# Depthwise-separable 1x1 layer on one core: the second weight load moves to ScalarE's queue, and the fourth weight piece is evicted by two engines

## The chip, the cores and the metric

The kernel runs on one core of one Trainium2 chip. The metric is device time in microseconds (us). Before the change three runs took 573.55, 574.01 and 574.22 us; their median is 574.01 us.

## The reference

x is a 1x384x384x384 image in bf16 (384 channels), dw a depthwise filter with a 1x1 window, pw a 384x384 matrix. With a window of one, the reference is

```python
out = x * dw[0, 0][None, None, None, :]       # one factor per channel
return jnp.einsum('bhwc,cd->bhwd', out, pw)
```

So the kernel computes x · (diag(dw) · pw), with x taken as 147,456 rows of 384 channels. The factor of each channel can be put into the weights once, ahead of the rows.

## The kernel before

**The rows.** The 147,456 rows are cut into 288 supertiles of 512 rows. Chunks of 1 to 10 supertiles are loaded by SyncE's queue (`load_x`, L121; the DMA is issued at L133) into three buffers X. The first chunks hold one supertile each (384 KB), so that the first can start early. VectorE transposes each supertile into T (L364 for the first half of the very first one, in three steps; L366 for all others). TensorE multiplies T by the weights w_r into a PSUM tile of four banks (`supertile`, L212; the matmul is at L222, 48 of them for a supertile). ScalarE evicts the PSUM tile into O (L426), and SyncE's queue stores O (L173). Two T tiles and two PSUM tiles, PS[0] and PS[1], alternate.

**The weights.** Before the first supertile the weights have to be built. w_r holds diag(dw) · pw with its rows in the order that the transposes give. dw (768 bytes) is loaded by ScalarE's queue (L178), and pw by SyncE's queue in two transfers: rows 0 to 127 (L179, 96 KB, semaphore s_pw) and rows 128 to 383 (L180, 192 KB, s_pw2). The first x chunk follows behind them on the same queue (L181, issued at L133). TensorE runs matmuls on constants while it waits (`idle_work`, L239), spreads dw over the partitions with three matmuls (L252), and VectorE copies the result (L394) and multiplies a selection matrix by it (L397), once for each k, which counts up s_sw.

Then TensorE makes the weights in six pieces i = 0 to 5, with k = i // 2 the 128 rows of pw and r = i % 2 (the loop at L263 to L280; the matmul is at L272). A piece is one pair of matmuls, v = 0 and 1, each into a PSUM bank of its own, and counts up s_w. The two pieces of k = 2 run their pair twice (`times`, L262). The pieces 0, 1, 4 and 5 lie in PS[1], the pieces 2 and 3 in PS[0] (`w_ps`, L206). Before k = 0 TensorE waits for s_pw, before k = 1 for s_pw2 (L265), and before each piece of k = 2 for the eviction of the piece that lies in the same banks (L269).

**The evictions of the weights.** `w_out` (L379) copies a piece of 128x768 from PSUM into w_r at L382: VectorE takes piece 1, ScalarE the pieces 0, 2, 3, 4 and 5, as `w_eng` (L175) says. s_wr[0] counts VectorE's, s_wr[1] ScalarE's.

**What the first supertile waits for.** It writes PS[0], where the pieces 2 and 3 have been. `w_first` (L204) makes TensorE wait for pieces 0 to 3 before step (0, 0), for piece 4 before step (4, 0) and for piece 5 before step (4, 1). Step (0, 0) also waits for the first transpose of L364, and that for the first x chunk.

**Order on the engines.** On ScalarE: the load of dw, the activation table and two tiny copies (L338), the evictions of the weights, then one eviction (L426) for each supertile. On VectorE: L387, L394, L397, the eviction of piece 1, then the transposes. GpSimd waits for all of w_r (`w_all`), then copies parts of it (L330) for the last supertile alone.

Of the kernel before, what the change touches and what calls it, by code (L numbers as in the profile page):

```python
# [26 lines left out]
def kernel(  # L27
# [12 lines left out]
    nc = tc.nc  # L40
    P = nc.NUM_PARTITIONS
    B, H, W, C = x.shape
# [31 lines left out]
    pw_n = raw[:, 0 : 3 * D].rearrange("p (k d) -> p k d", d=D)  # L74
# [4 lines left out]
    w_r = consts.tile([P, NB, 2, D], BF16, name="w_r")  # L79
# [25 lines left out]
    s_pw2 = nc.alloc_semaphore("s_pw2")  # L105
# [5 lines left out]
    s_wr = [nc.alloc_semaphore(f"s_wr{e}") for e in range(2)]  # L111

    with tc.tile_critical(sync_engine=mybir.EngineType.Pool, no_gpsimd_drain=True) as section:
# [7 lines left out]
        def load_x(t, eng=nc.sync):  # L121
            g, i, off, first, L = chunks[t]
            dst, sem, _ = x_of(t)
            rows = xf[512 * first : 512 * (first + L), :]
            if first + 3 < NS:
                src = rows.rearrange("(p s) c -> p (s c)", p=P)
                dst = dst.rearrange("p s c -> p (s c)")
                if i == 0 and g >= NR:
                    je = g_end[g - NR]
                    eng.wait_ge(s_t[je % 2][1], je // 2 + 1)  # L130
            else:
                src = rows.rearrange("(a k q) c -> q a k c", k=4, q=4)
            eng.dma_start(dst, src).then_inc(sem, 16)  # L133
# [38 lines left out]
            eng = nc.scalar if first + 1 == NS and k == 2 else nc.sync  # L172
            eng.dma_start(dst, src).then_inc(s_o[g % NR], 16)  # L173

        w_eng = [1, 0, 1, 1, 1, 1]  # L175
        w_all = [(s_wr[e], w_eng.count(e)) for e in range(2)]

        nc.scalar.dma_start(dw_row[:], dw.rearrange("a e c -> a (e c)")).then_inc(s_dw, 16)  # L178
        nc.sync.dma_start(pw_n[:, 0], pw[0:P, :]).then_inc(s_pw, 16)  # L179
        nc.sync.dma_start(pw_n[:, 1:3], pw[P:C, :].rearrange("(k p) d -> p k d", p=P)).then_inc(s_pw2, 16)  # L180
        load_x(0)  # L181

        todo = []
# [15 lines left out]

        w_done = [(s_wr[e], w_eng[: i + 1].count(e)) for i, e in enumerate(w_eng)]

        w_first = {(0, 0): [(0, 1), (1, 3)], (4, 0): [(1, 4)], (4, 1): [(1, 5)]}  # L204

        def w_ps(i):  # L206
            return PS[0 if i in (2, 3) else 1][:, 2 * (i % 2) : 2 * (i % 2) + 2, :D]
# [4 lines left out]
        def supertile(s, rv):  # L212
            for b, par in steps:
                for q in range(4):
                    if q == 0 and par == 0 and b in (0, 3):
                        nc.tensor.wait_ge(s_t[s][b // 3], rv)
                    if q == 0 and s == 0:
                        for e, v in w_first.get((b, par), []):
                            nc.tensor.wait_ge(s_wr[e], v)
                        if par == 0 and b in (1, 2):  # L220
                            nc.tensor.wait_ge(s_tb, b)
                    mm = nc.tensor.matmul(  # L222
                        PS[s][:, q, :D],
                        lhsT=Ts[s][32 * q : 32 * q + 32, b, par::2],
                        rhs=w_r[32 * q : 32 * q + 32, b, par, :],
                        start=(b, par) == steps[0],
                        stop=(b, par) == steps[-1],
                        tile_position=(32 * q, 0),
                    )
                    if (b, par) == steps[0] and q == 0:  # L230
                        mm._wait_ge(s_a[s], rv)
                    if (b, par) in ((2, 1), (5, 1)) and q == 3:
                        mm.then_inc(s_pe)
# [29 lines left out]
        for k in range(3):  # L263
            if k == 1:
                nc.tensor.wait_ge(s_pw2, 16)  # L265
            nc.tensor.wait_ge(s_sw, k + 1)
            for r in range(2):
                if k == 2:
                    nc.tensor.wait_ge(*w_done[r])  # L269

                for v in [0, 1] * times.get((k, r), 1):
                    mm = nc.tensor.matmul(  # L272
                        PS[(k + 1) % 2][:, 2 * r + v, :D],
                        lhsT=sel_w[64 * v : 64 * v + 64, k, r, :, :].rearrange("p q w -> p (q w)"),
                        rhs=pw_n[64 * v : 64 * v + 64, k, :],
                        start=True,
                        stop=True,
                        tile_position=(64 * v, 0),
                    )
                mm.then_inc(s_w)  # L280
        with nc.tensor.Fori(0, NS // 2 - 1, 1) as it:
            rv = nc.tensor.to_reg(it + 1)
            for s in range(2):
                supertile(s, rv)
        supertile(0, NS // 2)

        Tk = Ts[1][:].rearrange("p b (i r) -> p (b i) r", r=2)
# [15 lines left out]
        for m in range(4):  # L303
# [14 lines left out]
            out=eye[:],  # L318
            in_=ones[:, 0:P],
# [20 lines left out]
        def transposes(t, j):  # L340
            g, i, off, first, L = chunks[t]
            jj = first + j
            s = jj % 2
            if jj + 1 == NS:
                nc.vector.wait_ge(s_xk, 32)
                Tw = Ts[s][:].bitcast(U32).rearrange("p b (m w) -> p (b m) w", w=32)
                for v in range(2):
                    blocks = slice(12 * v, 12 * v + 12)
                    ins = nc.vector.transpose(out=Tw[:, blocks], in_=Xk[:, blocks].bitcast(U32))  # L349
                    ins._wait_ge(s_pe, 2 * (jj - 2) + v + 1)  # L350
                    ins.then_inc(s_t[s][v])
                return
            X, sem, n = x_of(t)
            Xw = X.bitcast(U32).rearrange("p (k l) c -> p k l c", l=L)
            Tw = Ts[s][:].bitcast(U32).rearrange(
                "p b (k i) -> p b k i" if t < 2 else "p b (i k) -> p b k i", k=4
            )
            for h in range(2):
                if h == 0 and j == 0:
                    nc.vector.wait_ge(sem, n)  # L360
                if h == 0 and jj == 0:
                    for b in range(3):
                        x_b = Xw[:, :, 0, 32 * b : 32 * b + 32]
                        nc.vector.transpose(out=Tw[:, b], in_=x_b).then_inc(s_tb if b else s_t[0][0])  # L364
                    continue
                ins = nc.vector.transpose(  # L366
                    out=Tw[:, 3 * h : 3 * h + 3],
                    in_=Xw[:, :, j, 96 * h : 96 * h + 96].rearrange("p k (b w) -> p b k w", w=32),
                )
                if jj >= 2:  # L370
                    ins._wait_ge(s_pe, 2 * (jj - 2) + h + 1)
                ins.then_inc(s_t[s][h])
# [3 lines left out]

        order = [(t, j) for t in range(NT) for j in range(chunks[t][4])]

        def w_out(i):  # L379
            e, k, r = w_eng[i], i // 2, i % 2  # L380
            out, in_ = w_r[:, 2 * k : 2 * k + 2, r, :], w_ps(i)
            o = nc.vector.tensor_copy(out, in_) if e == 0 else nc.scalar.copy(out, in_)  # L382
            o._wait_ge(s_w, i + 1)
            o.then_inc(s_wr[e])
# [3 lines left out]
            out=sel[:],  # L388
            in_=eye[:].rearrange("p (v w r) -> p r w v", v=2, r=2),
# [6 lines left out]
        for k in range(3):  # L396
            nc.vector.tensor_scalar_mul(  # L397
                sel_w[:, k], sel[:].unsqueeze(2).to_broadcast([P, 2, 4, 32]), dw_f[:, k : k + 1]
            ).then_inc(s_sw)
        for i in range(6):  # L400
            w_out(i)
        transposes(*order[0])
        transposes(*order[1])

        for jj, (t, j) in enumerate(order):
            g, i, off, first, L = chunks[t]
# [32 lines left out]
        for o in sorted(range(NR), key=lambda o: (len(groups) - 1 - o) % NR):  # L439
            n = sum(n_parts[t] for t, c in enumerate(chunks) if c[0] % NR == o)  # L440
# [36 lines left out]
```

## Time and profile before

| what | value |
|---|---|
| runs, median (lowest to highest) | 574.01 us (573.55 to 574.22) |
| the profiled execution's own time | 573.57 us |
| span of its profile, first to last instruction | 571.8 us |
| granted TensorE clock | 1.00 |
| TensorE matmul busy | 566.9 us (99%) |
| VectorE busy | 507.7 us (89%) |
| ScalarE busy | 418.7 us (73%) |
| GpSimd busy | 13.9 us (2%) |
| moved by DMA | 226.88 MB, mean 397 GB/s |

The profile shows one execution. Its times are counted from the first instruction of the span. PE is TensorE's matmul, PEld its weight load, DVE VectorE, ACT ScalarE, POOL GpSimd; SPq and ACTq are the issues of DMAs by SyncE and ScalarE. In a row of the timeline the first number is the start, the second the duration, and behind the operation stands, in brackets, how long the engine sat idle before it and what ended that. Times are in us unless ns is said. A matmul's duration reaches from its start to its modelled end, so that durations of matmuls overlap; the distance between starts tells the pace.

### The profile page before, as it was taken

What the parts mean: (1) busy time and instruction counts of PE and PEld (TensorE: products, weight loads), DVE (VectorE), ACT (ScalarE), POOL (GpSimd) and SP (SyncE); (2) the same over time, 40 slices, a digit from 0 to 9 for tenths busy, and PEclk for the clock granted to TensorE, in tenths of its full rate; (3) what the DMA queues carried; (4) which work ended last, traced back from release to release, by engine and by line L of the source; (5) the groups of instructions that cost most, each with busy time, mean ns of one, the idle gap of its engine ahead of it and who ended that gap; (6) DMA issues with size and microseconds to landing.
All of it is one profiled execution on the core that took longest, in us unless ns stands there. A gap on an engine that the chain in (4) does not pass through costs nothing.

```text
span 571.8 us, 29716 instructions
## 1 busy us (share of the span) xinstructions
PE 566.9 (99%) x13843; PEld 414.2 (72%) x13843; DVE 507.7 (89%) x588; ACT 418.7 (73%) x298; POOL 13.9 (2%) x41
## 2 busy tenths in 40 slices
PE   9999999999999999999999999999999999999997
PEld 5777777777777777777777777777777777777775
DVE  7888989989989989989989889889889889889885
ACT  6777777777777777777777777777777777777775
POOL 2042000000000000000000000000000000000000
PEclk9999999999999999999999999999999999999999
DMA  8999999999999999999999999999999999998677
GB/s 317 441 385 385 428 430 432 437 421 414 427 441 422 427 384 422 403 381 392 433 393 383 414 414 406 412 399 420 420 375 435 386 392 397 416 396 361 283 287 260
DMA packets 28085, 226.88 MB, mean 397 GB/s; under 512 B 1450, under 2 KB 7851, under 8 KB 24107
## 3 DMA queue, kind: packets, MB, share of 16 engines
q1 hardware_dynamic: 27140, 225.91, 97.5%
q10 hardware_dynamic: 934, 0.89, 0.4%
q14 instruction: 10, 0.07, 0.0%
q8 instruction: 1, 0.02, 0.0%
HBM read 113.54 MB, written 113.25 MB: 397 GB/s over the span
## 4 chain that ended last, share of the span: by engine, by line
PE 99%; issue 0%; ACT 0%
PE ps L222 98%; PE ps L272 0%; PE ps L239 0%; PE ps L307 0%; PE ps L295 0%; ACT O L421 0%; PE ps L252 0%
## 5 line engine op out<-in xcount | busy, mean ns | idle before, releaser
L222 PE MATMUL ps<-w_r,T 32*128 32x384 bf16 x13776 | 559.8, 321 | 0.1
L366 DVE STREAM_TRANSPOSE T<-X 128x384 uint32<-128x384 uint32 x571 | 499.8, 877 | 55.0 <-PE ps L222 1.1
L222 PEld LDWEIGHTS ps<-w_r,T 32*128 32x128 bf16 x13776 | 411.4, 93 | 148.6 <-issue 0.6
L426 ACT CAST O<-ps 128x1536 bf16<-128x1536 f32 x286 | 411.7, 1440 | 146.4 <-PE ps L222 146.4
L336 POOL COPY Xk<-Xl 32x256 bf16<-32x256 bf16 x16 | 6.3, 396 | 0.0
L335 POOL COPY Xk<-Xl 32x128 bf16<-32x128 bf16 x16 | 4.6, 290 | 25.6 <-DMA Xl<-in_x_dram 24.7
L382 ACT CAST w_r<-ps 128x768 bf16<-128x768 f32 x5 | 3.6, 818 | 0.8 <-PE ps L272 0.8
L330 POOL COPY raw<-w_r 32x768 bf16<-32x768 bf16 x4 | 3.3, 821 | 6.4 <-ACT w_r L382 6.2
L239 PE MATMUL ps<-const-bfloat16-1.0 32*128 32x384 bf16 x24 | 2.2, 516 | 1.1 <-PEq L461 1.1
L272 PE MATMUL ps<-raw 64*128 64x384 bf16 x16 | 2.8, 498 | 0.1
L272 PEld LDWEIGHTS ps<-raw 64*128 64x128 bf16 x16 | 0.8, 114 | 2.2 <-DMA raw<-in_pw_dram 1.2
L338 ACT ACT_TABLE_LOAD x1 | 1.3, 1283 | 1.5 <-PEq L461 1.5
L417 DVE CAST O<-ps 128x384 bf16<-128x384 f32 x2 | 1.0, 552 | 1.4 <-PE ps L222 1.4
L366 DVE STREAM_TRANSPOSE T<-Xl 128x384 uint32<-128x384 uint32 x2 | 1.8, 876 | 0.2
L239 PEld LDWEIGHTS ps<-const-bfloat16-1.0 32*128 32x128 bf16 x24 | 0.7, 117 | 1.5 <-issue 1.5
L387 DVE TENSOR_REDUCE sel<-eye 128x64 f32<-128x128 bf16 x1 | 0.3, 288 | 1.5 <-POOL eye L317 1.5
L349 DVE STREAM_TRANSPOSE T<-Xk 128x384 uint32<-128x384 uint32 x2 | 1.2, 578 | 0.5 <-PE ps L222 0.4
L421 ACT CAST O<-ps 128x384 bf16<-128x384 f32 x2 | 1.0, 479 | 0.7 <-PE ps L307 0.7
L307 PE MATMUL ps<-raw,T 128*128 128x384 bf16 x8 | 1.5, 327 | 0.0
L382 DVE CAST w_r<-ps 128x768 bf16<-128x768 f32 x1 | 1.0, 958 | 0.5 <-PE ps L272 0.5
L364 DVE STREAM_TRANSPOSE T<-X 128x128 uint32<-128x128 uint32 x3 | 0.7, 283 | 0.6 <-DMA X<-in_x_dram 0.6
L421 DVE CAST O<-ps 128x384 bf16<-128x384 f32 x2 | 1.1, 558 | 0.1
(14 smaller groups left out, 5.4 us busy)
## 6 DMA issues: line engine op xcount, KB each, us to landing
X<-in_x_dram SPq DMA_DIRECT2D x25, 3840.0 KB, 22.2
out_dram<-O SPq DMA_DIRECT2D x25, 3840.0 KB, 28.1
X<-in_x_dram SPq DMA_DIRECT2D x3, 1536.0 KB, 18.8
X<-in_x_dram SPq DMA_DIRECT2D x2, 1920.0 KB, 15.7
out_dram<-O SPq DMA_DIRECT2D x2, 1920.0 KB, 24.4
out_dram<-O SPq DMA_DIRECT2D x2, 1536.0 KB, 13.3
X<-in_x_dram SPq DMA_DIRECT2D x6, 384.0 KB, 5.2
out_dram<-O SPq DMA_DIRECT2D x3, 768.0 KB, 6.1
```

What stands on the lines that cost most here:

```text
L222: mm = nc.tensor.matmul(PS[s][:, q, :D], lhsT=Ts[s][32 * q : 32 * q + 32, b, par::2], rhs=w_r[32 * q : 32 * q + 32, b, par, :], start=(b, ...
L239: nc.tensor.matmul(PS[0][:, 2 * (i % 2) + i // 2, :D], lhsT=ones[32 * i : 32 * i + 32, 0:P], rhs=ones[32 * i : 32 * i + 32, :], start=True ...
L272: mm = nc.tensor.matmul(PS[(k + 1) % 2][:, 2 * r + v, :D], lhsT=sel_w[64 * v : 64 * v + 64, k, r, :, :].rearrange("p q w -> p (q w)"), rhs ...
L307: mm = nc.tensor.matmul(PS[1][:, m, :D], lhsT=Tk[:, P * (m + 2) : P * (m + 3), par], rhs=w_k[:, par, :], start=False, stop=par == 1,)
L330: nc.gpsimd.tensor_copy(w_k[quads[n]], w_r[quads[n], n]).then_inc(s_wk)
L335: nc.gpsimd.tensor_copy(Xk[quads[n], g:8:4, :], x_b).then_inc(s_xk)
L336: nc.gpsimd.tensor_copy(Xk[quads[n], 8 + g : 24 : 4, :], Xl[quads[g], :, 64 * n : 64 * n + 64]).then_inc(s_xk)
L338: nc.scalar.copy(warm[:, s : s + 1], nc.const_aps.tensor(0.0, [P, 1], F32)).then_inc(s_a[s])
L366: ins = nc.vector.transpose(out=Tw[:, 3 * h : 3 * h + 3], in_=Xw[:, :, j, 96 * h : 96 * h + 96].rearrange("p k (b w) -> p b k w", w=32),)
L382: o = nc.vector.tensor_copy(out, in_) if e == 0 else nc.scalar.copy(out, in_)
L421: o = (nc.scalar.copy if n % 2 else nc.vector.tensor_copy)(Ov[:, n, j, :], PS[s][:, n, :D])
L426: a = nc.scalar.copy(Ov[:, :, j, :], PS[s][:, :, :D])
```

## The change

Two things are changed. The second load of pw is issued by ScalarE's queue, behind dw, and no longer by SyncE's between the first load of pw and the first x chunk. And the fourth piece of the weights (i = 3) is evicted in two halves of one PSUM bank each, the first by ScalarE, the second by VectorE; the counts on which TensorE and GpSimd wait are worked out from the new list.

```diff
-        w_eng = [1, 0, 1, 1, 1, 1]
-        w_all = [(s_wr[e], w_eng.count(e)) for e in range(2)]
+        w_units = [(0, 0, 2, 1), (1, 0, 2, 0), (2, 0, 2, 1), (3, 0, 1, 1), (3, 1, 2, 0), (4, 0, 2, 1), (5, 0, 2, 1)]
+
+        def w_after(i):
+            n = [sum(u[3] == e and u[0] <= i for u in w_units) for e in range(2)]
+            return [(s_wr[e], n[e]) for e in range(2)]
+
+        w_all = w_after(5)
 
         nc.scalar.dma_start(dw_row[:], dw.rearrange("a e c -> a (e c)")).then_inc(s_dw, 16)
         nc.sync.dma_start(pw_n[:, 0], pw[0:P, :]).then_inc(s_pw, 16)
-        nc.sync.dma_start(pw_n[:, 1:3], pw[P:C, :].rearrange("(k p) d -> p k d", p=P)).then_inc(s_pw2, 16)
+        nc.scalar.dma_start(pw_n[:, 1:3], pw[P:C, :].rearrange("(k p) d -> p k d", p=P)).then_inc(s_pw2, 16)
         load_x(0)
...
-        w_done = [(s_wr[e], w_eng[: i + 1].count(e)) for i, e in enumerate(w_eng)]
-
-        w_first = {(0, 0): [(0, 1), (1, 3)], (4, 0): [(1, 4)], (4, 1): [(1, 5)]}
+        w_first = {(0, 0): w_after(3), (4, 0): w_after(4)[1:], (4, 1): w_after(5)[1:]}
...
-                        for e, v in w_first.get((b, par), []):
-                            nc.tensor.wait_ge(s_wr[e], v)
+                        for sem, v in w_first.get((b, par), []):
+                            nc.tensor.wait_ge(sem, v)
...
-                    nc.tensor.wait_ge(*w_done[r])
+                    nc.tensor.wait_ge(*w_after(r)[1 - r])
...
-        def w_out(i):
-            e, k, r = w_eng[i], i // 2, i % 2
-            out, in_ = w_r[:, 2 * k : 2 * k + 2, r, :], w_ps(i)
+        def w_out(i, v0, v1, e):
+            k, r = i // 2, i % 2
+            out, in_ = w_r[:, 2 * k + v0 : 2 * k + v1, r, :], w_ps(i)[:, v0:v1]
...
-        for i in range(6):
-            w_out(i)
+        for u in w_units:
+            w_out(*u)
```

A unit is (piece, first bank, last bank + 1, engine), with engine 0 VectorE and 1 ScalarE.

## The prediction, made before the result was known

> **What bounds the kernel now.** I read the page first (its groups), then the chain that ended last, then the timeline of each engine over the first 9 us in narrow windows, then the DMA view in windows. First the page's group of the main matmul and the chain:
>
> ```profile
> span 571.8 us, 29716 instructions
> L222 PE MATMUL ps<-w_r,T 32*128 32x384 bf16 x13776 | 559.8, 321 | 0.1
> ```
>
> ```profile
> 1.12 1.49 PE ps L239 x13
> ...
> 4.86 1.33 PE ps L272 x8
> 6.19 0.07 issue
> 6.26 559.83 PE ps L222 x13776
> ```
>
> The group's last number is TensorE's idle time ahead of these 13,776 matmuls: 0.1 us in all. From 6.26 to 566.09 nothing but TensorE's own pace counts (559.83 / 13,776 is 0.0406 us each, 0.1625 for four). The change touches only what lies ahead of 6.26. So the question is one: when does the first L222 start? Whatever it moves by moves the end by the same.
>
> Who ends last ahead of 6.26? The weights: ACT's and DVE's evictions, the first transpose, and PE's pairs of L272.
>
> ```profile
> 3.91 0.80 ACT L382 CAST w_r<-ps 128x768 bf16<-128x768 f32 x1 [0.80 <-PE ps L272]
> 4.61 0.80 ACT L382 CAST w_r<-ps 128x768 bf16<-128x768 f32 x1
> 5.30 0.82 ACT L382 CAST w_r<-ps 128x768 bf16<-128x768 f32 x1
> ```
>
> ```profile
> 4.23 0.96 DVE L382 CAST w_r<-ps 128x768 bf16<-128x768 f32 x1 [0.48 <-PE ps L272]
> 5.81 0.31 DVE L364 STREAM_TRANSPOSE T<-X 128x128 uint32<-128x128 uint32 x1 [0.62 <-DMA X<-in_x_dram]
> ```
>
> ```profile
> 3.37 0.82 PE L272 MATMUL ps<-raw 64*128 64x384 bf16 x4
> 3.96 0.87 PE L272 MATMUL ps<-raw 64*128 64x384 bf16 x4
> 4.86 0.82 PE L272 MATMUL ps<-raw 64*128 64x384 bf16 x4
> 5.45 0.74 PE L272 MATMUL ps<-raw 64*128 64x384 bf16 x4
> ```
>
> Three things end almost together: piece 3 is in w_r at 5.30 + 0.82 = 6.12, the first transpose is done at 5.81 + 0.31 = 6.12, and PE's last pair is issued at 5.77 (a row below), which at the pairs' distance of 0.32 frees PE at 6.09. The change is aimed at the first two. The third stands 0.17 behind 6.26. That is all that can be won, 0.03% of the time.
>
> **The change, part by part.**
>
> *The halves.* Single-bank evictions stand at the kernel's end:
>
> ```profile
> L421 ACT CAST O<-ps 128x384 bf16<-128x384 f32 x2 | 1.0, 479 | 0.7 <-PE ps L307 0.7
> L421 DVE CAST O<-ps 128x384 bf16<-128x384 f32 x2 | 1.1, 558 | 0.1
> ```
>
> ACT's half would end at 5.30 + 0.48 = 5.78 instead of 6.12. DVE's half starts behind piece 1 (4.23 + 0.96 = 5.19) and takes 0.56, to 5.75; DVE lay idle there (the 0.62 in the row at 5.81), so it costs nothing as long as x is not there before. Alone, this part wins 0.34 for piece 3 and, with the 6.12 of the transpose and the 6.09 of PE beside it, next to nothing for the start. ACT's pieces 4 and 5 come 0.34 earlier; steps (4, 0) and (4, 1) do not wait for them now, as the 0.1 us of idle says. GpSimd's copies (L330) feed only the end of the kernel.
>
> *The queues.* Before, with ACT's first compute instruction:
>
> ```profile
> 0.97 0.39 SPq L179 DMA_DIRECT2D raw<-in_pw_dram  x1
> 1.42 0.41 SPq L180 DMA_DIRECT2D raw<-in_pw_dram  x1
> 1.88 0.46 SPq L133 DMA_DIRECT2D X<-in_x_dram  x1
> ```
>
> ```profile
> 0.97 0.53 ACTq L178 DMA_DIRECT2D dw_row<-in_dw_dram  x1
> 1.54 1.28 ACT L338 ACT_TABLE_LOAD   x1 [1.54 <-PEq L461]
> ```
>
> ```profile
> raw<-in_pw_dram SPq DMA_DIRECT2D x1, 192.0 KB, 2.5
> X<-in_x_dram SPq DMA_DIRECT2D x1, 384.0 KB, 3.9
> ```
>
> Without L180 on SP, the first x chunk is issued at 1.42, 0.46 earlier, and so are the x chunks behind it. On ACT the load of pw comes behind dw at 0.97 + 0.53 = 1.50, 0.08 later than before, and takes 0.41 to 0.53. It pushes the table load and the two small copies by 0.4 to 0.5; ACT was idle for 0.80 ahead of its first eviction at 3.91, so 0.3 is left and nothing is lost. dw itself stays first.
>
> *What the new queue does to the transfer* is the term that decides. Before, pw's 192 KB stood ahead of all x in one queue and landed at 1.42 + 2.5 = 3.92; k = 1 started at 3.96, just as PE came free. Now pw's packets are in ACT's queue and x's are in SP's, ready at the same moment. How the 16 DMA engines share two queues is seen later in this trace, where Xl (ACT's queue, 384 KB) meets a long transfer of SP's. The DMA view of 28 to 31 us, and the wait that it ended:
>
> ```profile
> q1 hardware_dynamic: 40, 1.23, 97.6%
> q10 hardware_dynamic: 42, 0.06, 5.7%
> ```
>
> ```profile
> 24.05 0.42 ACTq L137 DMA_DIRECT2D Xl<-in_x_dram  x1
> ```
>
> ```profile
> 35.87 0.29 POOL L335 COPY Xk<-Xl 32x128 bf16<-32x128 bf16 x1 [24.75 <-DMA Xl<-in_x_dram]
> ```
>
> 40 packets of SP's queue (q1, 30 KB each) against 42 of ACT's (q10, 1.5 KB each): one for one, whatever their size. 384 KB took 11.8 us in that company, against 3.9 for the first x chunk. For pw: 256 rows of 768 bytes (k = 1 and 2 over 128 partitions) are 256 packets, 16 for each engine. An x chunk of one supertile is 128 packets of 3 KB, 8 for each engine. So pw lands when 16 x packets of each engine have gone between, the whole first and second chunk. Their pace, from three DMA windows, 1.8 to 2.5, 2.5 to 3.5 and 4.5 to 7.0 us:
>
> ```profile
> q1 hardware_dynamic: 128, 0.09, 50.2%
> ...
> DMA packets 295, 0.23 MB, mean 233 GB/s; under 512 B 22, under 2 KB 285, under 8 KB 295
> ...
> DMA packets 315, 0.85 MB, mean 339 GB/s; under 512 B 39, under 2 KB 39, under 8 KB 315
> ```
>
> The 128 packets of the first pw load are all begun by 2.5. Of the second window, 285 - 22 = 263 packets are pw's: 16.4 for each engine in 1 us, 0.06 each. Of the third, 315 - 39 = 276 are x's: 17.25 in 2.5 us, 0.145 each. A pair costs 0.145 + 0.06 = 0.205; the low end is 0.175 (the small one half hidden beside the large), the high end 0.22. 16 pairs from 2.5 take 3.3 us (2.8 to 3.5), and the last packets, begun by 3.5, landed at 3.92, so 0.4 more. pw then lands at 6.1 to 6.2 (5.7 to 6.4) instead of 3.92. I take 6.15: 2.2 us later.
>
> *From there.* Call the start of k = 1 T = 6.2. PE has six pairs left (two of k = 1, four of k = 2), none of which waits for an eviction any more, since pieces 0 and 1 are long in w_r. At 0.32 they are through at T + 1.92 = 8.12. ACT: piece 2 starts at T + 0.6 and its half of piece 3 0.7 later, done at T + 1.8. DVE: its half starts when piece 3 is made, T + 0.9, done T + 1.45, the transpose T + 1.75 (x, after 8 pairs, landed at 2.5 + 1.65 + 0.4 = 4.55). So PE's pairs end last, all three within 0.2, and the halves save 0.2 that the unsplit piece 3 would have cost. First L222: 8.1 instead of 6.26, **+1.85**.
>
> *The clock.* The matmuls' pace changes once in the trace, though the granted clock is shown as 1.00 throughout:
>
> ```profile
> 5.45 0.55 PE L272 MATMUL ps<-raw 64*128 64x384 bf16 x2
> ...
> 5.77 0.42 PE L272 MATMUL ps<-raw 64*128 64x384 bf16 x2
> ```
>
> A matmul of 384 columns takes 0.52 up to here, then 0.4, and 0.32 at L222, where pairs' pace has doubled. It happens at about 5.8, 4.7 us after the first matmul at 1.12. The new wait leaves PE idle from 3.37 + 0.82 = 4.19 to 6.2. Nothing in the trace shows a matmul after an idle stretch like that, so two bounds. If the full pace comes at 5.8 all the same, the six pairs go at half the distance, the evictions set the start at about T + 1.65, and 0.25 is won back. If the 4.7 us count anew from T, full pace comes at 10.9, and the L222 from 8.1 to 10.9 run at half pace: 1.4 lost. I take the middle, **+0.5**. [...]
>
> *Sum.* 1.85 + 0.5 = +2.35, from the profiled execution's 573.57 (span 571.8 and 1.77 around it) 575.9. That execution lies 0.44 under the median of 574.01, at the lower end of its runs; on the median the sum is 576.3, which I forecast. Its own range is 575.1 (pw at 5.7, clock as before: +1.35 - 0.25 = +1.1) to 577.5 (+2.1 + 1.4).
>
> **Rivals.**
>
> *A. pw is not held up* (it enters the engines before x does, or the sharing is kinder at the start than at 28 us). Then the change does what it says: x lands at 5.35, DVE's half ends at 5.75, the transpose at 6.06, and PE's 6.09 sets the start: -0.17, 573.85, no slower. It decides up to a delay of 0.3: k = 2 starts at 4.86 for ACT's piece 0 (3.91 + 0.80), and k = 1 could end 0.3 later without being noticed. For it: both loads are issued within 0.1 us. Against it: 16 packets need 1 us even alone, and x's stand ready all that time.
>
> *B. The engines take longer turns than one packet*, so that pw's 16 packets of an engine go through in one turn, behind the first x chunk: 2.5 + 8 x 0.145 + 16 x 0.06 + 0.4 = 5.0, first L222 at 5.05 + 1.92 = 7.0, +0.7, 574.7 (with the clock between 574.5 and 575.3). Against it: the 40 to 42. [...]
>
> *C. x gets a whole chunk's lead.* It is issued 0.08 ahead of pw. If the engines take x's first 8 packets before pw's first, 24 of x's pass before pw lands, not 16: 8 x 0.145 = 1.2 more, +3.5 with the clock's middle and +4.4 with its upper bound, 577.5 to 578.4. Against it: the first x packets stand behind the first pw load until 2.5, so that 0.08 should be lost there.
>
> **How the numbers follow.** The forecast has 0.74, A 0.10, B 0.10, C 0.06. The range for 8 in 10 takes in the forecast's own (575.1 to 577.5) and B: 574.5 to 577.5; A and C stay outside. A measurement of this kernel can tell about 0.2%, 1.15 us, from no change; slower by more means over 575.16. That is nearly all of the forecast, all of C and a little of B: 0.78. Within 0.2%: A, most of B and the edge of the forecast: 0.21. Faster by over 0.2%: no case reaches it, 0.01.
>
> **What the profile after would show.** Right: the weight load ahead of k = 1 waits over 1.5 us for pw's DMA; pw's 192 KB take 4.0 to 5.0 from issue to landing; ACTq's packets stand one for one against SPq's in the first 6 us; the first x chunk lands before pw; the first L222 starts at 7.7 to 8.5; the group of L222 lasts 559.8 or up to 1.4 more. Wrong: k = 1 still starts at about 4.0 (A), or at about 5 (B); or L222 shows idle time of its own, so that something behind the start has changed, which I exclude above.

## The result and the profile after

Six runs of the changed kernel took 575.16 to 577.31 us, median 576.10; six of the kernel before, beside them, 573.55 to 574.22, median 573.86. The ratio is 1.0042 with a 95% interval of 1.0028 to 1.0055: 1.6 to 3.2 us slower. The profiled execution took 575.75, 2.18 more than that of before.

The page's first line and main group, and the chain that ended last:

```profile
span 574.0 us, 29717 instructions
L225 PE MATMUL ps<-w_r,T 32*128 32x384 bf16 x13776 | 560.7, 321 | 0.0
```

```profile
1.53 4.00 DMA raw<-in_pw_dram
5.53 0.05 issue
5.58 2.10 PE ps L275 x12
7.68 560.59 PE ps L225 x13304
```

The main matmul stands at L225 now, that of the weights at L275. The chain, which before began with TensorE's own matmuls, now has a transfer ahead of them: pw's 192 KB from 1.53 to 5.53. Then come the six pairs of matmuls and the supertiles. (The chain lacks some records of L225; in the timeline the first one stands at 7.61.)

```profile
7.61 4.58 PE L225 MATMUL ps<-w_r,T 32*128 32x384 bf16 x88
```

Two terms make up the 2.2 us of the span: the first L225 starts at 7.61 instead of 6.26 (1.35), and the group lasts 560.7 instead of 559.8 (0.9). The rows of the stretches show where the 0.9 lies. Each has in brackets how many matmuls were under way in 0.8 us of TensorE's time; first the changed kernel, then the kernel before (where the second bracket counts the weight loads):

```profile
8.50:9.30 0.80, 0.80 (x16) 1.00 1.01 407
9.30:10.10 0.80, 0.80 (x28) 1.00 1.21 499
```

```profile
7.06:7.86 0.80, 0.80 (x28) 0.60 (x20) 1.00 0.97 373
```

28 matmuls in a stretch is the full pace, 16 about half of it. Before, the first supertile ran at full pace; now its first 1.7 us run at half. The clock column says 1.00 in both, but ahead of the first change it shows nothing: the trace lists the changes of the clock, and what lies ahead of the first entry counts as 1.00. That entry is at 5.92 before and at 9.34 after. In e5 below the list has a fall as well, and there 16 matmuls in a stretch go with 0.50 and 28 with 1.00.

The evictions of the changed kernel, ScalarE's and VectorE's, and the first transpose:

```profile
3.91 0.80 ACT L385 CAST w_r<-ps 128x768 bf16<-128x768 f32 x1 [0.36 <-PE ps L275]
6.12 0.80 ACT L385 CAST w_r<-ps 128x768 bf16<-128x768 f32 x1 [1.42 <-PE ps L275]
6.82 0.48 ACT L385 CAST w_r<-ps 128x384 bf16<-128x384 f32 x1
```

```profile
6.44 0.56 DVE L385 CAST w_r<-ps 128x384 bf16<-128x384 f32 x1 [1.26 <-PE ps L275]
6.92 0.30 DVE L367 STREAM_TRANSPOSE T<-X 128x128 uint32<-128x128 uint32 x1
```

Both engines now sit idle for 1.3 to 1.4 us until TensorE has made piece 2 and piece 3, and all is ready by 7.3. ScalarE's first eviction is still at 3.91: issuing the load in front of it cost nothing, 0.36 of idle time is left.

How the two queues shared the DMA engines, from 2.5 to 3.8 and from 3.8 to 4.5 us (q1 is SyncE's queue, q10 ScalarE's):

```profile
q1 hardware_dynamic: 117, 0.31, 82.6%
q10 hardware_dynamic: 1, 0.00, 0.2%
...
q10 hardware_dynamic: 207, 0.16, 66.5%
q1 hardware_dynamic: 45, 0.10, 34.6%
```

First x almost alone, then mostly pw: 207 packets against 45, with two thirds of the engines' time against one third. Though the load was issued only 0.11 behind x's, its first packets came 2.3 us after its issue, when the first x chunk had nearly gone through (103 of its 128 packets begun by 3.8).

### The profile page after: what moved, and what is told of

The parts are those of the page before. It is cut to its first block, busy times and chain, and to the rows that moved or that the text cites. A ratio compares the mean times of both kernels' runs of the same rounds, so it can differ in the third digit from the quotient of the medians.

```text
span 574.0 us, 29717 instructions
## 1 busy us (share of the span) xinstructions
PE 567.7 (99%) x13843; PEld 337.1 (59%) x13843; DVE 510.2 (89%) x589; ACT 418.3 (73%) x298; POOL 13.9 (2%) x41
## 4 chain that ended last, share of the span: by engine, by line
PE 98%; DMA 1%; ACTq 0%; ACT 0%; issue 0%; POOLq 0%
PE ps L225 98%; DMA raw<-in_pw_dram 1%; PE ps L275 0%; PE ps L310 0%; PE ps L298 0%; ACTq L183 0%; ACT O L424 0%; ACTq L475 0%; POOLq L113 0%; POOLq L464 0%
## 5 line engine op out<-in xcount | busy, mean ns | idle before, releaser
L225 PE MATMUL ps<-w_r,T 32*128 32x384 bf16 x13776 | 560.7, 321 | 0.0
L225 PEld LDWEIGHTS ps<-w_r,T 32*128 32x128 bf16 x13776 | 334.4, 93 | 226.5 <-issue 1.5
L385 ACT CAST w_r<-ps 128x768 bf16<-128x768 f32 (+1 forms) x5 | 3.4, 746 | 1.8 <-PE ps L275 1.8
L275 PE MATMUL ps<-raw 64*128 64x384 bf16 x16 | 2.9, 515 | 1.5 <-DMA raw<-in_pw_dram 1.4
L385 DVE CAST w_r<-ps 128x768 bf16<-128x768 f32 (+1 forms) x2 | 1.5, 758 | 1.7 <-PE ps L275 1.7
L275 PEld LDWEIGHTS ps<-raw 64*128 64x128 bf16 x16 | 0.9, 125 | 3.5 <-DMA raw<-in_pw_dram 2.8
```

The costliest lines, as they stand in the source:

```text
L225: mm = nc.tensor.matmul(PS[s][:, q, :D], lhsT=Ts[s][32 * q : 32 * q + 32, b, par::2], rhs=w_r[32 * q : 32 * q + 32, b, par, :], start=(b, ...
L275: mm = nc.tensor.matmul(PS[(k + 1) % 2][:, 2 * r + v, :D], lhsT=sel_w[64 * v : 64 * v + 64, k, r, :, :].rearrange("p q w -> p (q w)"), rhs ...
```

## The experiments

**Theory.** The late landing of pw delays k = 1, and that alone sets the time, in two ways: the later start, and half pace in the first supertile because TensorE sat idle ahead of it. **Rivals:** the split eviction costs the time; ScalarE's queue is slow in itself; the half pace has nothing to do with the idle stretch.

The table has every kernel that ran. The median of the kernel before, from runs taken alongside, stands in brackets; the last four columns are from the profiled execution: when pw's 192 KB landed, the first main matmul, the length of its group, and the span.

| kernel | median (before) | ratio, 95% | pw landed | first | group | span |
|---|---|---|---|---|---|---|
| before | 573.86 | | 3.92 | 6.26 | 559.8 | 571.8 |
| changed | 576.10 (573.86) | 1.0042, 1.0028 to 1.0055 | 5.53 | 7.61 | 560.7 | 574.0 |
| e1 queue alone | 576.11 (573.92) | 1.0036, 1.0024 to 1.0048 | 5.82 | 8.05 | 560.2 | 573.9 |
| e2 split alone | 573.59 (573.92) | 0.9995, 0.9983 to 1.0006 | 3.8 | 6.46 | 559.8 | 572.0 |
| e3 x held | 574.39 (573.92) | 1.0006, 0.9997 to 1.0015 | 5.12 | 7.20 | 560.7 | 573.6 |
| e4 PE busy | 575.96 (573.92) | 1.0027, 1.0016 to 1.0038 | 6.17 | 7.92 | 559.8 | 573.4 |
| e5 pw held | 579.01 (573.83) | 1.0082, 1.0065 to 1.0099 | 9.47 | 11.55 | 561.3 | 578.6 |
| e6 changed again | 575.97 (573.83) | one run | 5.20 | 7.29 | 561.2 | 574.2 |
| e7 wait alone | 576.48 (573.83) | 1.0047, 1.0030 to 1.0063 | 4.4 | 8.13 | 560.7 | 574.5 |
| e8 PE busy again | 576.75 (573.83) | one run | 5.74 | 7.49 | 559.8 | 575.0 |
| e9 PE busy, short | 575.16 (573.83) | 1.0022, 1.0013 to 1.0031 | 5.5 | 7.71 | 559.8 | 573.2 |
| e10 split again | 573.92 (573.83) | 1.0000, 0.9991 to 1.0009 | 3.9 | 6.46 | 560.2 | 572.5 |

In every row but e8's the span is 571.8, plus what the first matmul is later than 6.26, plus what the group is longer than 559.8, within 0.15. So in these profiles the two terms are the whole of it.

**e1, the queue alone.** The changed kernel with the old evictions:

```diff
-        w_units = [(0, 0, 2, 1), (1, 0, 2, 0), (2, 0, 2, 1), (3, 0, 1, 1), (3, 1, 2, 0), (4, 0, 2, 1), (5, 0, 2, 1)]
+        w_units = [(0, 0, 2, 1), (1, 0, 2, 0), (2, 0, 2, 1), (3, 0, 2, 1), (4, 0, 2, 1), (5, 0, 2, 1)]
```

> The queue is moved, piece 3 is evicted whole by ScalarE as before. Theory (the late landing of pw sets the time): k = 1 starts at 5.5 to 5.7 as after the whole change; ScalarE ends piece 3 about 0.35 later, so that the first L222 comes 0.1 to 0.2 later; total +2.0 to +2.6 us against the kernel before. Rival (the split eviction costs the time, with two engines on one PSUM tile): within 0.3 us of the kernel before.

Measured: +2.2, as the theory has it. Its chain:

```profile
1.53 4.29 DMA raw<-in_pw_dram
5.82 0.05 issue
5.86 2.10 PE ps L275 x12
7.96 0.09 issue
8.05 560.16 PE ps L225 x13776
```

In this execution pw landed 0.3 later than in the changed kernel's, so k = 1 starts at 5.86, past the 5.5 to 5.7 expected. From there to the first main matmul it takes 2.19 where the split version took 2.03, so between these two profiles the split saves 0.16.

**e2 and e10, the split alone.**

```diff
-        nc.scalar.dma_start(pw_n[:, 1:3], ...)
+        nc.sync.dma_start(pw_n[:, 1:3], ...)
```

> pw's last 256 rows stay in SyncE's queue, piece 3 is evicted in halves. Theory: piece 3 is ready at about 5.8, the first transpose still ends at 6.12 and sets the start; 0 to -0.1 us, not to be told from the kernel before. Rival (the split costs the time): +1 us or more.

> Split evictions alone, pw in SyncE's queue, a second set of runs to see whether it beats the kernel before. Theory: piece 3 is no longer what the first L222 waits for, but the first transpose ends at the same moment, so 0 to -0.3 us, ratio 0.9995 to 1.0000. Rival (a real gain by the split): -0.5 us or more.

Measured: 0.9995 and 1.0000, both within what can be told from no change. The first of the two shows why; its chain:

```profile
1.88 4.14 DMA X<-in_x_dram
6.02 0.02 issue
6.04 0.32 DVE T L367
6.37 0.09 issue
6.46 559.83 PE ps L225 x13776
```

The wait has gone to the next one in line, the landing of the first x chunk. No version was found that beats the kernel before. (e10's profile has a group of 560.2, 0.4 more than the kernel before, with no idle stretch like that of the changed kernel: the doubling of the pace comes late there by itself, at 7.35 by the clock's first entry.)

**e3, x held back.**

```diff
+        nc.sync.wait_ge(s_dw, 16)
         load_x(0)
```

> The whole change, but SyncE waits until dw has landed (about 2.24) before it issues the first x chunk, so that pw is in its queue about 0.8 us ahead of x. Theory (x, issued ahead of pw, goes first through the DMA engines): pw lands at 3.6 to 4.1, k = 1 starts by 4.1, total -0.2 to +0.3 us. Rival (ScalarE's queue is slow to begin a transfer, whoever is ahead): pw still lands after 5.0, total +1.5 us or more.

Measured: +0.5, with an interval of -0.2 to +0.9; that is 1.7 below the changed kernel. The size was missed: the profiled execution is the slowest of e3's eleven (575.38, the next 574.68), and in it pw still landed only at 5.12, which is the rival's number:

```profile
1.53 3.59 DMA raw<-in_pw_dram
...
7.27 560.65 PE ps L226 x13776
```

The queues of the same profile, from 2.5 to 3.5 and from 4.5 to 5.1 us, tell the two apart:

```profile
DMA packets 209, 0.15 MB, mean 154 GB/s; under 512 B 11, under 2 KB 208, under 8 KB 209
q10 hardware_dynamic: 188, 0.14, 62.6%
...
q10 hardware_dynamic: 7, 0.00, 2.3%
```

Up to 3.5 most of the packets of pw's 192 KB go, and only one of x's (the one packet that is not under 2 KB). The last seven of ScalarE's queue come past 4.5, behind x, and the landing waits for them. So x, issued first, is what held pw up, and not ScalarE's queue in itself. When pw landed in the other ten runs no profile shows.

**e5, pw held back.** If the engines share in a fixed manner, it should show when x has a longer lead:

```diff
+        nc.scalar.wait_ge(s_dw, 16)
         nc.scalar.dma_start(pw_n[:, 1:3], ...)
```

> The whole change, but ScalarE waits until dw has landed (about 2.24) before it issues pw's 192 KB: issue at about 2.3, behind the first two x chunks of SyncE's queue and beside the third. Theory (an engine that turns to ScalarE's queue takes all 16 packets of pw in one go, after the x chunk that it is at): pw lands at 5.3 to 5.9 as after the change, total +2.0 to +2.6 us. Rival 1 (one packet for one): 16 pairs of 0.2 us from 3.4 on, landing at about 7.0, total +3.3 to +4.5 us, with q1 and q10 packets side by side in the windows. Rival 2 (the engines keep the order of issue over both queues): pw comes in one go but behind two or three x chunks, landing at 6.5 to 7.5, total +3 to +4.5 us.

Measured: +5.2, outside all three; the profiled execution is the slowest of the four (580.39, the others 577.53 to 579.49). The chain, and the queues from 3.4 to 4.8, 5.0 to 7.0 and 7.0 to 9.0 us:

```profile
2.32 7.15 DMA raw<-in_pw_dram
...
11.62 561.28 PE ps L226 x13772
```

```profile
q1 hardware_dynamic: 169, 0.47, 105.4%
...
q1 hardware_dynamic: 119, 0.33, 55.4%
q10 hardware_dynamic: 147, 0.11, 21.3%
...
q1 hardware_dynamic: 207, 0.68, 91.2%
q10 hardware_dynamic: 119, 0.08, 13.1%
```

Issued at 2.32, pw gets not one packet until 4.8; then the queues go about one for one, and the last packet comes at 9. Here the sharing of the prediction does appear, behind a wait for x that had been queued before. My theory of one turn falls as a general rule.

TensorE sits idle from 4.19 to 9.52 here, and this is the one profile whose clock falls while matmuls are still to come. Two stretches of 0.8 us of the first supertile:

```profile
13.22:14.02 0.80, 0.80 (x16) 0.50 1.16 495
14.82:15.62 0.80, 0.80 (x28) 1.00 1.11 476
```

The list of clock changes has full clock from 4.44, half from 7.85 and full again from 14.68. Of the 6.8 us by which this span is longer than that of before, 5.3 are the later start and 1.5 the half clock.

**e7, the wait alone.** The kernel before, with nothing but the late start put in:

```diff
             if k == 1:
                 nc.tensor.wait_ge(s_pw2, 16)
+                nc.tensor.wait_ge(x_of(0)[1], 16)
```

> The kernel before, both loads of pw in SyncE's queue, whole evictions; only TensorE waits before k = 1 until the first x chunk has landed (5.4 to 6.0), as it waits for pw after the change. Theory (all of the loss comes from the late start of k = 1 and the idle stretch ahead of it): k = 1 starts at 5.5 to 6.0, the pace doubles after 8, total +2.0 to +2.7 us. Rival (the queue itself or ScalarE's later start costs a part of the time): +1.3 us or less.

Measured: +2.65. The chain:

```profile
4.41 1.53 issue
5.94 2.10 PE ps L273 x12
8.05 0.08 issue
8.13 560.71 PE ps L222 x13116
```

Both loads in the old queue, old evictions, and the whole loss is there: 1.9 from the start and 0.9 from the pace. (k = 1 starts at 5.94 here, 0.36 later than in the changed kernel's profile.)

**e6, the changed kernel again.**

> The changed kernel once more, for a second profile. Theory (the spread of its times of 2.2 us comes from when the last engine's share of pw lands and from when the pace of the matmuls doubles): the landing and the moment of the doubling differ from the first profile (5.53 and about 9.3), and the span follows the sum of the two, within 0.2 us.

Measured: pw lands 0.33 earlier, yet the span is 0.2 longer, because half pace lasts longer: the group takes 561.2, and the stretch from 9.30 to 10.10 still has 16 matmuls.

```profile
9.30:10.10 0.80, 0.80 (x16) 1.00 1.19 492
10.10:10.90 0.80, 0.80 (x24) 1.00 1.03 438
```

So one part of the spread of the changed kernel's times is the landing, another the moment at which the pace doubles.

**e4, e8 and e9, TensorE kept busy.** e4 and e8 are one kernel; e9 (the second half of the diff) fills the idle stretch with 5 matmuls of 128 rows instead of 20 of 32; the filler takes 1.4 us in e4's profile, 1.1 in e8's and 1.8 in e9's. What they write is overwritten by k = 1:

```diff
             if k == 1:
+                idle_work(5)
                 nc.tensor.wait_ge(s_pw2, 16)
...
             if k == 1:
+                for i in range(5):
+                    nc.tensor.matmul(PS[0][:, i % 4, :D], lhsT=ones[:, 0:P], rhs=ones, start=True, stop=True)
                 nc.tensor.wait_ge(s_pw2, 16)
```

> The whole change, and TensorE runs 20 matmuls on constants (about 1.6 us) between k = 0 and k = 1, where it sits idle after the change. Theory (the idle stretch puts off the full pace of the matmuls): the pace doubles at about 5.8 as in the kernel before, the first L222 starts at 7.2 to 7.5 at full pace, total +1.0 to +1.3 us. Rival (the full pace comes at a moment that does not depend on the idle stretch): total +2.0 to +2.4 us as after the change.

> The changed kernel with the 20 matmuls on constants between k = 0 and k = 1, once more, for a second profile. Theory: the pace of the matmuls doubles ahead of the first L222 here too, and the span is that of the kernel before plus what the first L222 starts later. Rival (the first profile had the early doubling by luck, and the runs at 576.0 to 576.4 did not have it): the pace doubles after 8.

> The whole change, and between k = 0 and k = 1 TensorE runs 5 matmuls of the full 128 rows on constants (about 1.6 us), 5 instructions with their weight loads in place of 20. Theory (the idle stretch costs 0.8 to 1.5 us by the late doubling of the pace, and the runs of the kernel with 20 matmuls at 576.0 and above lost some 2 us at their end by a further load of instructions, which fewer instructions avoid): pace doubled ahead of the first L222, group of L222 at 559.8, no load of instructions on q8 near the end, nearly all runs between 574.6 and 575.4, total +1.0 to +1.4 us. Rival (filling the idle stretch gains nothing in the end): total +2.0 us or more.

In all three profiles the group is back at 559.8: full pace from the first main matmul on. e9's chain:

```profile
3.37 0.82 PE ps L277 x4
4.20 1.72 PE ps L269 x5
5.91 0.45 PE ps L277 x2
6.36 0.02 issue
6.39 1.19 ACT w_r L387 x2
7.58 0.14 issue
7.71 559.83 PE ps L225 x13776
```

The pairs go at full pace too (12 matmuls take 1.15 us in e4 and e8 and 1.38 in e9, against 2.10), so that ScalarE's evictions come last ahead of the start, no longer TensorE. e9 takes +1.3, as expected, and about 0.3 of that is its own: the filler holds k = 1 back to 5.9, and pw had landed at 5.5. The time of e4 missed its expectation: +2.0, though its profile has +1.6. By the time alone it lies in the rival's range; it is the profile, at full pace from the first main matmul on, that speaks against the rival. pw landed at 6.17 in it, so that the first main matmul came at 7.92 and not at 7.2 to 7.5. e8 shows what can happen there; the DMA view of 570 to 571.9 us, and its last store:

```profile
q8 instruction: 1, 0.02, 4.6%
...
out_dram<-O ACTq DMA_DIRECT2D x1, 96.0 KB, 3.8
```

A load of instructions falls among the last stores, and the last one takes 3.8 us to land instead of 1.9: the 2 us by which e8's span exceeds its two terms. The load's packet takes 1.4 us from 571.02 on (4.6% of 16 engines over 1.9 us), and 18 packets of the stores, 9 of each queue, begin only behind it, from 572.4 on. The kernel before has one such load, early; e4, e8 and e9 have a second one, which in the profiles of e4 and e9 comes after the span has ended. That e4's six runs of 575.96 to 576.38 have the same cause, and that e9 has no run above 575.66 because it adds fewer instructions, is not shown: no profile of such a run of e4 was taken. Those six have a mean granted clock of 0.997 or 0.998, e4's other five 1.000 and e8 0.999, so a fall of the clock as in e5 is a rival. And without any filler, 7 of the 34 runs of the kernel before that stand beside e1 to e4 took 575.1 to 576.0.

## Why the prediction was right, and where not

- **The bound** (all depends on when the first main matmul starts): right. Start and pace of the first supertile add up to the span in eleven of twelve profiles.
- **The halves** (worth next to nothing): right. Alone they give 0.9995 and 1.0000; beside the late pw they save 0.16, where 0.2 was said.
- **ScalarE's own delay** (hidden, 0.3 left): right, 0.36 left.
- **How the queues share** ("one for one", pw at 6.15): this step failed. pw landed at 5.53 in the first profile, and in the others with the same loads at 5.20 (e6), 5.82 (e1), 6.17 (e4), 5.74 (e8) and 5.5 (e9), 0.2 to 1.2 later than rival B's sum but in B's order: the first x chunk went nearly through (in the first profile 103 of its 128 packets begun by 3.8), then pw's packets came almost in one go. Even in e4, whose 6.17 is the predicted number, 231 of pw's 256 packets had begun by 5.0. The row from 28 to 31 us was a true one, but it shows a stretch 4 us behind Xl's issue at 24.05, and from 24 to 28 q10 had 2 packets against 58 of q1; e5 shows about one for one at the start too (119 of q1 against 147 of q10 from 5.0 to 7.0), once several x chunks stand queued ahead. Turns of more than one packet agree with the 207 packets of q10 against 45 of q1 from 3.8 to 4.5, and not with e5.
- **The 0.06 for a packet of pw**: one count was slightly misread. Of the 128 packets of SyncE's queue up to 2.5 us, 8 are of 4 bytes, where a row of pw has 768, so 8 packets of the first load were still to come, and 255 of the 263 behind are the second load's. It changes next to nothing.
- **From k = 1 to the first main matmul** (T + 1.92): right; 5.58 + 1.92 = 7.50, measured 7.61.
- **The start in sum**: +1.35 instead of +1.85, by the landing alone.
- **The clock** (+0.5, between -0.25 and +1.4): the direction was right, the size low: 0.9 in the first profile, 1.4 in the second, 0.9 in e3 and e7, 0.4 in e1, 0 where the idle stretch was filled, and 0.4 once without one (e10). The full clock came at 8.77 to 10.14 in the five profiles with an idle stretch of 1.0 to 1.7 us, and at 4.30 to 7.35 in the six without one of that length. In e5 it came at 4.44, just after the idle stretch had begun, and was lost again at 7.85, so that the price seems to depend on where the change falls against the idle stretch. In the two profiles of the changed kernel it came at 9.34 and at 10.14; no run shows what sets that moment.
- **The sum**: 1.35 + 0.9 = 2.25 against 1.85 + 0.5 = 2.35. The 576.3 came close to 576.1 because two errors of opposite sign, 0.5 and 0.4, nearly cancelled: that is luck.
- **Its signs**: the weight load waited for pw's DMA, pw took 4.0 us from issue to landing, x landed first and the group lasted 0.9 longer, all as said. The packets were not one for one, and 7.61 lies just below 7.7 to 8.5; k = 1 at 5.58 lies between the forecast's 6.2 and B's 5.05.
- **Rival A** (x lands earlier, slightly faster): did not happen. x landed at about 5.0 instead of 5.8, but had nothing to feed.

What stays open: what decides whether ScalarE's packets go in one burst or one for one after x's, and why they wait for x chunks that were issued ahead. The runs show both, not the rule. Nor do they show how much idle time it takes to put off the full clock.

## What to carry to other kernels

In these runs a second queue was no second road: a transfer that was needed early lost its place when it left the queue in which it stood in front, and waited for what had been issued ahead of it on the other (pw landed at 5.53 instead of 3.92). Before a load is moved to bring another one forward, ask which of the two is needed first; here the one was needed at 3.9 and the other at 5.8. And a wait of TensorE ahead of its full pace cost more than its length here: 1.35 us of later start brought another 0.9 of half pace, and 1.03 brought 1.4 in a second execution. Where the wait was filled with matmuls it brought none, in three profiles.

## What the runs showed of the hardware that was not expected

- Half pace of the matmuls after an idle stretch of only 1.0 to 1.7 us (from 4.19 to the start of k = 1 in e3 and e1; group 560.2 to 561.2 instead of 559.8), while the clock column, which has no entry yet, says 1.00 in the stretch where 16 matmuls run in place of 28. After 5.3 us idle (e5) the column does show 0.50, for 6.8 us.
- The order of issue on two queues matters over tenths of a microsecond: 0.11 behind x, pw's first packets came 2.3 us after their issue; 0.9 behind, about 2.5 us, and the last at 9 us; ahead of x (e3), 1.1 us.
- A load of 16 KB of instructions among the last stores of the kernel went with 2 us in one profile (last store 3.8 us to land instead of 1.9). A second load appears with 20 matmuls more in the program (e4, e8) and also with 5 (e9); in e4 and e9 it comes after the end.
